# TensorE's branch behind a 448-token slot, 30 products sooner

## The chip, the cores and the metric

The kernel runs on one core of a Trainium2 chip. The metric is the device time of one execution in microseconds (us). A core has five engines with instruction queues of their own: TensorE (PE; its weight loads are listed as PEld), VectorE (DVE), ScalarE (ACT), GpSimd (POOL) and SyncE (SP), which starts most of the DMAs. A name with a q behind it (PEldq, DVEq) is an instruction that the engine's sequencer handles itself: a branch, a wait, a load of a register.

## The reference

Two steps, for 8 batches of 12 heads, 448 tokens and 64 columns per head:

```python
attn = sigmoid(q @ k.T / sqrt(64) - log(448))         # no softmax
x = (attn @ v) as [3584 tokens, 768]
e = argmax(x @ w_gate); gate_w = softmax(x @ w_gate)[e]
eom = sigmoid(x @ w_output_gate)[e]                   # of the token's expert
out = gate_w * eom * (relu(x @ w1[e]) @ w2[e])        # w1: 768 x 1024, w2: 1024 x 768
```

Each token goes to one of 8 experts. How many tokens an expert has is known only while the kernel runs.

## The kernel before

**Stages.** Up to about 268 us the kernel computes the attention, batch by batch, and at the side the gates and a list of tokens for each expert. Then it works the lists off in slots. A slot is a group of tokens of one expert: 448 (`TB`) in a full slot, 240 (`TM`) in a half slot. Two full slots take their tokens from the lists as they stand before the last batches are done, so that their loads start early; two more always follow, and up to eight more follow where the lists need them; what is left of each expert goes into half slots. With the inputs here there are seven full slots and two half slots.

**A full slot** (`slot`) has two layers. Layer 1 makes h = relu(x @ w1) in 8 parts of 128 columns. Every operand is split in a high and a low part of a shorter format, by ScalarE (high) and VectorE (low), and a product of two such operands takes three products on TensorE: L479, L480 and L481 in `products`, where the high and low part of the tokens lie side by side and the rest, which no longer fits in a bank of PSUM, is added up by VectorE in `join` (L485, L486). Layer 2 (`layer2_columns`, `layer2_turned`) makes y = h @ w2 with the columns of y as rows of PSUM, in six groups c of 128 columns; a group is 8 steps f of 3 products, 24 products, and ends with `turn_back`, in which VectorE joins the rest and turns the block (L508). Group 4 goes to `self.psy` bank 3 and group 5 to bank 4 of PSUM. The turning back of groups 4 and 5, the writing of the rows to DRAM, loading them back by token, scaling them (L555) and scattering them (L562) are left to the next slot: `finish`, a generator that the next slot calls step by step. `self.left` hands the two PSUM tiles over.

**A half slot** has layer 1 with 240 tokens, as three separate products L467, L468 and L469 for each of the 6 steps, and layer 2 the other way round (L518 to L520).

**Order.** The order of every engine's instructions is that in which the Python issues them (`manual_schedule`). The engines wait for each other by counters (semaphores), which the framework sets from the tiles that the instructions read and write.

**Branches.** Behind the four fixed full slots stand eight conditional ones, nested: each is the Else of an If (L923) whose own block is empty, so that an engine either goes on into the next slot or leaves the whole nest for the first half slot. The count of slots is read from memory by each engine (L917, and L918 for the half slots). Every engine has a branch of its own, at its own place of the stream. TensorE's stands behind the last product of layer 2 of a slot. A branch can be announced by a hint: in `layer2_columns`, ScalarE's, VectorE's and GpSimd's are marked ahead of group 2, TensorE's ahead of group 5.

```python
            for k in range(LATE_MIN, LATE_MAX):
                with tc.If(full < k + 1, label=f"big{k}", preferred_fallthrough_block=False) as none:
                    pass
                ctx.enter_context(none.Else())
...
        self.left = self.left[0], None
        with tc.manual_schedule():
            half(0)
```

With the inputs here L923 is met four times: behind the fourth full slot, the fifth and the sixth the chain goes on, and behind the seventh it is left.

Of the kernel before, what the change touches and what calls it, by code (L numbers as in the profile page):

```python
# [52 lines left out]
def r32(ap):  # L53
    return ap.bitcast(F32)


class Kernel:
# [19 lines left out]
    def memory(self):  # L77
        self.rounded = self.pool("rounded").tile([128, ROUNDED // 4], F32R, name="rounded")
        self.plain = self.pool("plain").tile([128, PLAIN // 4], F32, name="plain")
        ps = self.pool("psum", space=PSUM).tile([128, 8, 512], F32, name="ps")  # L80
        self.ps_s = [ps[:, 0:2], ps[:, 2:4]]
        self.ps_o = [[ps[:, 4], ps[:, 5]], [ps[:, 6], ps[:, 7]]]
        self.ps_s2 = ps[:, 6:8]
        self.psh = [ps[:, i] for i in (0, 1, 2)]
        self.psy = [ps[:, i] for i in (4, 5, 3)]
        self.ps_step = ps[:, 3, 0:8]
        self.rot = {}
        self.beat = [None, None]
        self.hints = {2: [ET.Activation, ET.DVE, ET.Pool]}

        c = self.carve
        w = c(0, 3, 2, 2, DF)
        self.w1s = [[w[:, d // 2, a, d % 2] for d in range(6)] for a in range(2)]
        self.w1p = [[w[:, k, a] for k in range(3)] for a in range(2)]
        self.x2 = c(12 * DF * 4, 6, 2 * TB)
        self.xs = [self.x2[:, :, TB * i:TB * i + TB] for i in range(2)]
        self.slots_begun = 0

        self.w1r = c(0, 6, DF, dt=F32)
        self.w2r = c(0, 8, DM, dt=F32)  # L100
        self.xg = c(6 * DF * 4, GB_, Q4, dt=F32)
        self.xT = c(6 * DF * 4 + XG, 6, TB, dt=F32)
        self.yq = c(6 * DF * 4 + XG, GB_, Q4, dt=F32)
        self.xTm = c(6 * DF * 4 + XG, 6, 32 * GM, dt=F32)
        self.spare = c(6 * DF * 4 + GM * Q4 * 4, DM, dt=F32), c(6 * DF * 4 + XG + 6 * 32 * GM * 4, DM, dt=F32)
# [390 lines left out]
        self.beat[0] = nc.scalar.activation(hh, ps, AF.Relu).ins  # L496
        nc.vector.scalar_tensor_tensor(hl, ps, 0.0, r32(hh), ALU.max, ALU.subtract)  # L497

    def layer2_turned(self, c):
        ps = self.take("y", self.psy)  # L500
        for f in range(8):
            wh, wl = self.w2_at(f, slice(128 * c, 128 * c + 128))
            self.products(ps, wh, wl, self.h2[:, f], f == 0, f == 7)
        return ps
# [65 lines left out]
    def slot(self, cur, nxt, side=None, begun=False, hint=None):  # L570
        nx = None
        if nxt is not None:
            nx, rows, sure = nxt() if callable(nxt) else nxt
            last = -(-nx["lx"].shape[1] // 2) - 1
        n = 32 * cur["lx"].shape[1]
        lag = 0 if self.left is not None or n == TB else 2
        fin = self.finish(n)
        next(fin, None)
        self.rot["y"] = 1
        for f in range(8):  # L580
            if begun and f == 1:
                self.change_step()
            self.layer1(f, TB if n == TB else TM, begun and f == 0)
            if nx is not None and n < TB:
                if f >= lag:
                    self.gather_rows(nx, f - lag, rows, 1)
                if f == 7 and lag == 0:
                    self.nc.gpsimd.drain()
            elif nx is not None and f <= last:
                self.gather_rows(nx, 2 * f, rows, 1)  # L590
                self.gather_rows(nx, 2 * f + 1, rows, 0)
                if f == last and not sure:
                    self.nc.gpsimd.drain()
            if f == 6 and n < TB:
                next(fin, None)
            if side is not None:
                next(side, None)
            if 1 <= f < 5:
                self.split_w2(f - 1)
                if f > 1:  # L600
                    self.load_w1(nx, f - 2)
        if lag == 0:
            for k in range(3):
                self.turn_x(nx, k)
        if n == TB:
            next(fin, None)
            self.layer2_columns(cur, nx, side, hint, fin)
            self.slots_begun += 1
            return nx
        ws = {0: (0, 1), 1: (2,)}  # L610
        for i in range(4):
            t = i // 2
            self.layer2(cur, t, i % 2, self.ys[t])
            if nx is not None:
                if lag and i == 0:
                    for g in range(8 - lag, 8):
                        self.gather_rows(nx, g, rows, g % 2)
                    self.nc.gpsimd.drain()  # L618
                for k in ws.get(i, ()):
                    self.split_w1(k)  # L620
                    for j in range(k, 4 if k == 2 else k + 1):
                        self.load_w2(nx, j)
                if lag and i == 0:
                    for k in range(3):
                        self.turn_x(nx, k)
                if i < 3:
                    self.split_x(nx, i)
            if i < 2:
                next(fin, None)
            if side is not None:  # L630
                next(side, None)
            if hint is not None and i == 1:
                self.tc.mark_branch_hint_location(hint, hint="LikelyTaken", engines=[ET.SP])
        return nx

    def layer2_columns(self, cur, nx, side, hint, fin):
        for k in range(3):
            self.split_x(nx, k)
        ps = []
        for c in range(6):  # L640
            if hint is not None and c in self.hints:
                hinted = self.hints[c]
                more = self.nc.values_load(self.more[0:1, hint[1]:hint[1] + 1], engines=hinted, min_val=0, max_val=1)
                self.tc.mark_branch_hint_location(hint[0], hint=more, engines=hinted)
            if hint is not None and c == 5:
                self.tc.mark_branch_hint_location(hint[0], hint="LikelyTaken", engines=[ET.PE])
            ps.append(self.layer2_turned(c))
            if nx is not None and c < 3:
                self.split_w1(c)
                for j in range(c, 4 if c == 2 else c + 1):  # L650
                    self.load_w2(nx, j)
            if c < 4:
                self.turn_back(ps[c], c)
            if c in (0, 2):
                next(fin, None)
            if c == 0:
                lt = cur["lt"]
                self.nc.vector.tensor_copy(self.left_at, lt[:, :, 0])
                self.nc.vector.tensor_copy(self.left_w, r32(lt[:, :, 1]))
            if side is not None:  # L660
                next(side, None)
        self.left = ps[4:], cur["lt"]

    def attention(self, pool):
        nc = self.nc
# [311 lines left out]
```

## Time and profile before

| | us |
|---|---|
| median of 3 runs | 748.69 (747.67 to 748.84) |
| the profiled execution, its own time | 748.09 |
| its span, from the first to the last instruction | 746.3 |
| TensorE busy | 738.2 (99%), 5576 products |
| VectorE, ScalarE, GpSimd busy | 449.8, 370.1, 250.3 |
| mean granted clock of TensorE | 0.998 of 2.4 GHz |

The profile is that of one execution. An engine's busy share is its work over the span; a product's time is from its start to a modelled end, and products overlap, so the distance of two starts says what one costs. The waits of an engine, and what ended them, are inferred from the counters. Where an engine's sequencer waits or branches, its work stands still or runs out of its queue, and the profile doesn't count that as busy.

### The profile page before, as it was taken

What the parts mean: (1) busy time and instruction counts of PE and PEld (TensorE: products, weight loads), DVE (VectorE), ACT (ScalarE), POOL (GpSimd) and SP (SyncE); (2) the same over time, 40 slices, a digit from 0 to 9 for tenths busy, and PEclk for the clock granted to TensorE, in tenths of its full rate; (3) what the DMA queues carried; (4) which work ended last, traced back from release to release, by engine and by line L of the source; (5) the groups of instructions that cost most, each with busy time, mean ns of one, the idle gap of its engine ahead of it and who ended that gap; (6) DMA issues with size and microseconds to landing.
All of it is one profiled execution on the core that took longest, in us unless ns stands there. A gap on an engine that the chain in (4) does not pass through costs nothing. (4 is left out here: it accounts for less than half of the span.)

```text
span 746.3 us, 14692 instructions
## 1 busy us (share of the span) xinstructions
PE 738.2 (99%) x5576; PEld 543.0 (73%) x5576; DVE 449.8 (60%) x907; ACT 370.1 (50%) x437; POOL 250.3 (34%) x375
## 2 busy tenths in 40 slices
PE   9999999999999999999999999999999999999996
PEld 4334444444344369999999999999999999999996
DVE  1343863585777849936746746746655565656555
ACT  5666666566777734404514514514514333434644
POOL 5000130032354335247525315315225234233461
PEclk9999999999999999999999999999999999999999
DMA  9464656647595765367386386476386476576951
GB/s 307 138 194 148 195 138 192 195 119 209 179 325 178 213 138 178 127 163 214 118 293 217 123 273 216 132 267 208 142 274 184 176 243 205 187 247 191 322 198 46
DMA packets 90647, 145.76 MB, mean 195 GB/s; under 512 B 16738, under 2 KB 67298, under 8 KB 90560
## 3 DMA queue, kind: packets, MB, share of 16 engines
q1 hardware_dynamic: 79808, 119.22, 51.9%
q0 software_dynamic: 9680, 24.53, 9.4%
q10 hardware_dynamic: 1072, 0.92, 0.5%
q8 instruction: 46, 0.75, 0.4%
q14 instruction: 41, 0.34, 0.1%
HBM read 118.40 MB, written 32.62 MB: 202 GB/s over the span
## 5 line engine op out<-in xcount | busy, mean ns | idle before, releaser
L709 ACT ACTIVATE a<-ps,small 128x896 f32<-128x896 f32 x168 | 168.5, 1007 | 85.2 <-PE ps L707 83.0
L707 PE MATMUL ps<-q,k 64*64 64x448 f32 x1344 | 157.1, 540 | 0.0
L716 PE MATMUL ps<-a,v 64*64 64x448 f32 x1344 | 155.8, 536 | 0.0
L389 POOL DMA_INDIRECT plain<-x_dram,lxs x112 | 111.0, 991 | 132.3 <-ACT h L496 63.2
L496 ACT ACTIVATE h<-ps 128x448 fp32r<-128x448 f32 (+1 forms) x72 | 36.5, 506 | 206.7 <-DVE ps L486 129.9
L479 PE MATMUL ps<-h,w2h 128*128 128x512 f32 x336 | 130.7, 389 | 0.0
L481 PE MATMUL ps<-h,w2l 128*128 128x448 f32 x336 | 122.6, 365 | 0.0
L479 PE MATMUL ps<-rounded 128*128 128x512 f32 x288 | 112.0, 389 | 0.0
L480 PE MATMUL ps<-h,w2h 128*128 128x384 f32 x336 | 111.9, 333 | 0.0
L707 PEld LDWEIGHTS ps<-q,k 64*64 64x64 f32 x1344 | 49.9, 134 | 76.8 <-issue 70.0
L716 PEld LDWEIGHTS ps<-a,v 64*64 64x64 f32 x1344 | 50.6, 133 | 75.7 <-issue 72.1
L481 PE MATMUL ps<-rounded 128*128 128x448 f32 x288 | 105.1, 365 | 0.0
L415 DVE TENSOR_TENSOR rounded<-plain,rounded 128x2048 fp32r<-128x2048 f32 (+5 forms) x63 | 96.4, 1566 | 10.0 <-ACT rounded L414 8.9
L480 PE MATMUL ps<-rounded 128*128 128x384 f32 x288 | 95.9, 333 | 0.0
L414 ACT CAST rounded<-plain 128x2048 fp32r<-128x2048 f32 (+5 forms) x63 | 82.0, 1333 | 24.8 <-DVE plain L434 23.6
L485 DVE COPY hb<-ps 128x64 f32<-128x64 f32 x90 | 19.8, 220 | 103.3 <-PE ps L481 86.4
L562 POOL DMA_INDIRECT out<-y,lts x24 | 42.8, 1782 | 105.3 <-ACT y L555 102.3
L481 PEld LDWEIGHTS ps<-h,w2l 128*128 128x128 f32 x336 | 63.1, 188 | 13.2
L415 DVE TENSOR_TENSOR w2l<-plain,w2h 128x768 fp32r<-128x768 f32 x72 | 65.8, 954 | 3.4 <-ACT w2h L414 0.6
L497 DVE SCALAR_TENSOR_TENSOR h<-ps,h 128x448 fp32r<-128x448 f32 (+1 forms) x72 | 41.3, 574 | 42.6 <-ACT h L496 36.1
L480 PEld LDWEIGHTS ps<-h,w2h 128*128 128x128 f32 x336 | 63.1, 188 | 4.9
L479 PEld LDWEIGHTS ps<-h,w2h 128*128 128x128 f32 x336 | 63.1, 188 | 0.0
(164 smaller groups left out, 934.6 us busy)
## 6 DMA issues: line engine op xcount, KB each, us to landing
plain<-w SPq DMA_DIRECT2D x40, 768.0 KB
plain<-w SPq DMA_DIRECT2D x27, 1024.0 KB
k<-kT SPq DMA_DIRECT2D x23, 448.0 KB
q<-qT SPq DMA_DIRECT2D x23, 448.0 KB
x_dram<-xt SPq DMA_DIRECT2D x30, 336.0 KB
v<-vm SPq DMA_DIRECT2D x23, 384.0 KB
y<-y_dram SPq DMA_DIRECT2D x18, 384.0 KB
y_dram<-plain SPq DMA_DIRECT2D x28, 192.0 KB
```

The costliest lines, as they stand in the source:

```text
L389: self.paced(self.nc.gpsimd.indirect_dma_start(out=self.xg[:, g], out_offset=None, in_=x4, in_offset=bass.IndirectOffsetOnAxis(ap=s["lx"][ ...
L414: self.nc.scalar.copy(hi, raw)
L415: self.nc.vector.tensor_tensor(lo, raw, r32(hi), ALU.subtract)
L479: mm(ps, wh, both[:, 0:512], start=first, stop=False)
L480: mm(ps[:, 512 - TB:TB], wh, both[:, 512:2 * TB], start=False, stop=False)
L481: return mm(ps[:, 0:TB], wl, both[:, 0:TB], start=False, stop=last)
L496: self.beat[0] = nc.scalar.activation(hh, ps, AF.Relu).ins
L497: nc.vector.scalar_tensor_tensor(hl, ps, 0.0, r32(hh), ALU.max, ALU.subtract)
L562: i = self.nc.gpsimd.indirect_dma_start(out=self.out, out_offset=bass.IndirectOffsetOnAxis(ap=at, axis=0), in_=y, in_offset=None, bounds_c ...
L707: qk = nc.tensor.matmul(ps[half[h], j, 0:S], k[half[j], e, o:o + 64], q[half[j], e], start=True, stop=True)
L709: self.beat[0] = nc.scalar.activation(at[u % 3], ps[:, :, 0:S], AF.Sigmoid, bias=self.bias_s, scale=1.0 / math.sqrt(D)).ins
L716: nc.tensor.matmul(self.ps_o[e][h][half[j], 0:S], v[half[h], e, c, j], a[half[h], j], start=(i in ((0, 3 if h else 4)[e],)), stop=(i == (2 ...
```

## The change

Before, a full slot issues all six groups of layer 2 and its branch stands behind them. After, the slot ends with the steps f = 0 to 5 of group 4. The steps 6 and 7 of group 4 (6 products) and the whole of group 5 (24 products) are issued at the head of the next `slot` call, whichever it is: the next full slot or the first half slot. `self.open` tells that call that a group is open and in which tile; the tile of group 5 is taken there and added to the same list that `self.left` holds. TensorE's hint is marked ahead of group 4. The order of TensorE's products stays what it was; what moves against them is the branch of L923, the register loads of L917 and L918 and the hint.

```diff
+        self.open = None
...
-    def layer2_turned(self, c):
-        ps = self.take("y", self.psy)
-        for f in range(8):
+    def layer2_turned(self, c, fs=range(8), ps=None):
+        ps = self.take("y", self.psy) if ps is None else ps
+        for f in fs:
             wh, wl = self.w2_at(f, slice(128 * c, 128 * c + 128))
             self.products(ps, wh, wl, self.h2[:, f], f == 0, f == 7)
         return ps
...
         n = 32 * cur["lx"].shape[1]
         lag = 0 if self.left is not None or n == TB else 2
+        if self.open is not None:
+            self.layer2_turned(4, range(6, 8), self.open[0])
+            self.open.append(self.layer2_turned(5))
+            self.open = None
         fin = self.finish(n)
...
-            if hint is not None and c == 5:
+            if hint is not None and c == 4:
                 self.tc.mark_branch_hint_location(hint[0], hint="LikelyTaken", engines=[ET.PE])
-            ps.append(self.layer2_turned(c))
+            if c < 5:
+                ps.append(self.layer2_turned(c, range(6) if c == 4 else range(8)))
...
-        self.left = ps[4:], cur["lt"]
+        self.open = ps[4:]
+        self.left = self.open, cur["lt"]
```

## Rows read from the trace of the kernel before

**Rows 1.** The page, part 1: busy us (share of the span) and instructions.
```profile
PE 738.2 (99%) x5576; PEld 543.0 (73%) x5576; DVE 449.8 (60%) x907; ACT 370.1 (50%) x437; POOL 250.3 (34%) x375
```

**Rows 2.** Waits of TensorE, whole span: us in total, times, longest.
```profile
PE ps L798 <- DVE small L780: 0.9, 1, 0.9
PE ps L467 <- PEq L923: 0.6, 1, 0.6
```

**Rows 3.** Timeline of TensorE, 667 to 675 us: start, us, what, idle before.
```profile
667.11 0.36 PE L481 MATMUL ps<-h,w2l 128*128 128x448 f32 x1
...
673.11 0.37 PE L481 MATMUL ps<-h,w2l 128*128 128x448 f32 x1
674.03 0.35 PE L467 MATMUL ps<-rounded 128*128 128x240 f32 x1 [0.56 <-PEq L923]
```

**Rows 4.** Windows: busy us (instructions) of PE, PEld, DVE, ACT, POOL; clock, DMA, GB/s.
```profile
674.00:740.00 66.00, 65.82 (x480) 65.53 (x480) 41.29 (x54) 38.78 (x56) 28.44 (x23) 1.00 0.59 200
```

**Rows 5.** Line 923, 480 to 660 us: duration ns min/median/max, first and last start.
```profile
L923 PEldq COMPARE_BRANCH  x3: 73/81/95, 496.9 to 612.1; - x3
```

**Rows 6.** Line 923, 660 to 667.2 us.
```profile
L923 DVEq COMPARE_BRANCH  x1: 84/84/84, 664.5 to 664.5; - x1
L923 SPq COMPARE_BRANCH  x1: 133/133/133, 664.9 to 664.9; - x1
L923 ACTq COMPARE_BRANCH  x1: 69/69/69, 665.7 to 665.7; - x1
```

**Rows 7.** Line 923, 667.2 to 675.3 us.
```profile
L923 SPq EVENT_SEMAPHORE  x9: 17/17/17, 671.0 to 675.1; - x9
...
L923 PEldq COMPARE_BRANCH  x2: 200/283/366, 669.7 to 673.7; - x2
L923 DVEq EVENT_SEMAPHORE  x2: 21/21/21, 671.2 to 671.3; - x2
L923 ACTq EVENT_SEMAPHORE  x2: 17/17/17, 671.8 to 671.9; - x2
L923 DVEq COMPARE_BRANCH  x1: 61/61/61, 671.4 to 671.4; - x1
...
L923 PEldq EVENT_SEMAPHORE  x1: 51/51/51, 673.5 to 673.5; - x1
```

**Rows 8.** Windows, 668 to 673 us, columns as in rows 4.
```profile
668.00:673.00 5.00, 5.00 (x27) 4.52 (x26) 0.00 (x0) 0.00 (x0) 0.00 (x0) 1.00 0.97 342
```

**Rows 9.** Line 467, 660 to 680 us, and the same line, 700 to 740 us.
```profile
L467 PEldq EVENT_SEMAPHORE  x1: 51/51/51, 673.9 to 673.9; - x1
...
L467 PE MATMUL ps<-rounded x48: 271/274/278, 706.9 to 722.7; 128*128 128x240 f32 x48
```

**Rows 10.** Line 508, 670 to 690 us, and the same line, 600 to 667 us.
```profile
L508 DVEq EVENT_SEMAPHORE  x5: 21/50/50, 676.2 to 676.5; - x5
...
L508 DVE STREAM_TRANSPOSE plain<-ps x10: 649/649/651, 599.8 to 664.4; 128x448 f32<-128x448 f32 x10
```

**Rows 11.** Line 917, whole span: TensorE's load of the slot count.
```profile
L917 PEldq TENSOR_LOAD <-tot x1: 509/509/509, 439.3 to 439.3; - x1
```

**Rows 12.** Branch hints (filed at line 973), 480 to 740 us.
```profile
L973 PEldq BRANCH_PREFETCH_HINT  x3: 31/31/36, 497.1 to 612.3; - x3
```

**Rows 13.** Line 485, 670 to 690 us: VectorE's first work behind the exit.
```profile
L485 DVE COPY hb<-ps x2: 186/205/224, 675.9 to 677.2; 128x64 f32<-128x64 f32 x2
```

**Rows 14.** TensorE's last product (timeline), and windows of the span's end.
```profile
739.52 0.34 PE L520 MATMUL ps<-w2h,h 128*128 128x384 f32 x1
...
742.00:743.00 1.00, 0.00 (x0) 0.00 (x0) 0.00 (x0) 0.00 (x0) 0.00 (x0) 1.00 0.63 166
743.00:744.00 1.00, 0.00 (x0) 0.00 (x0) 0.00 (x0) 0.00 (x0) 0.00 (x0) 0.53 0.31 119
```

**Rows 15.** Line 707 at the start, 3 to 5.9 us, and 6 to 12 us.
```profile
L707 PE MATMUL ps<-q,k x12: 751/951/1006, 3.8 to 5.4; 64*64 64x448 f32 x12
...
L707 PE MATMUL ps<-q,k x40: 536/536/761, 5.3 to 11.2; 64*64 64x448 f32 x40
```

## The prediction

> **What bounds the kernel now.** I read the page first: TensorE is busy for 738.2 of the 746.3 us of the span [rows 1]. Then its waits: there are two in the whole execution, 0.9 us ahead of the first product and 0.6 us at L467 behind the branch of L923 [rows 2]. So TensorE is the path, and an edit can change the time only where it opens or closes a hole in TensorE's stream. The stream around that second wait, taken product by product, is the place of this change: the last product of layer 2 starts at 673.11, the first product of the first half slot at 674.03 [rows 3]. Products of a 448-token slot follow each other every 0.20 us (30 of them lie between the starts 667.11 and 673.11 [rows 3]), so 0.92 - 0.20 = 0.72 us is lost there. Behind it TensorE works 65.82 of 66.00 us up to the last product [rows 4]: nothing downstream can take up a delay, and none is there to be won.
>
> **The branch, passed and left.** L923 is passed four times here. Three times the chain goes on; TensorE's sequencer spends 73 to 95 ns on the branch [rows 5] and the engine has no wait there [rows 2]. The fourth time all engines leave for the first half slot. That is where the engines differ, and the views of L923 before and after 667.2 us show it. VectorE takes the branch at 664.5, SyncE at 664.9, ScalarE at 665.7 [rows 6], but their first instructions in the exit block are at 671.2, 671.0 and 671.8 [rows 7]: 6.7, 6.1 and 6.1 us in which their queues are empty, while the DMA engines are 97% busy [rows 8]. TensorE's branch is at 669.7, 3.4 us ahead of its last product's start, since its sequencer runs ahead of the array; its exit block's EVENT_SEMAPHORE is at 673.5 and its second branch at 673.7 [rows 7], just behind that product's end (673.11 + 0.37 [rows 3]). So TensorE empties its queue once and goes on half a microsecond later, and comes last of the three computing engines: VectorE and ScalarE have left their exit blocks by then.
>
> **What is filed behind the meeting point.** L923 has EVENT_SEMAPHOREs at this exit alone, on each engine ([rows 7]; the view of the three other passes, [rows 5], lists branches only). I take them for the instructions that bring the engines' counters to where the skipped slots would have left them. The rows behind them fit: the first product of the first half slot has an EVENT_SEMAPHORE ahead of it, while the 48 products of the same line in the second half slot have none (the second row is all that this view has beside weight loads [rows 9]); VectorE's turn back, L508, has five of them behind the exit and none in the ten instructions ahead of it [rows 10]. So an instruction behind the meeting point waits again for operands that its engine has long known to be ready, and, by my reading, until the engine that made them has gone through its own exit block.
>
> **The change, part by part.**
> *The 30 products.* They are the same instructions in TensorE's order, 30 x 0.20 = 6.00 us, and none is added. In the unconditional slots and at the three passes that go on nothing stands between them and what follows, so they cost nothing there; what hides the branch is the sequencer's lead of 3.4 us over the array, and the price without this cover is its 0.1 us [rows 5] each time.
> *TensorE's loads of the two slot counts* (L917, L918) come ahead of the 30 products. L917 takes 509 ns [rows 11], within the same lead: nothing.
> *The hint*, set ahead of column group 4 instead of 5: the three on TensorE are filed at 497.1 to 612.3 [rows 12], that is 0.2 us behind the branches at 496.9 to 612.1 [rows 5], at the head of the slot and not where the Python marks it. Nothing.
> *No DMA and no instruction of another engine moves*; VectorE's turn back of groups 4 and 5 stands in the next slot as before.
> *The exit.* Here the order tells. TensorE now stops behind the product that starts at 667.11 [rows 3]. Its branch comes 6.0 us sooner, about 663.7. Behind the meeting point stand first group 4's products of f = 6 and 7, which read h (high part by ScalarE, low part by VectorE) and w2 (the same two engines). If they wait again as L467 does, they wait until VectorE's counter (671.2 to 671.3) and ScalarE's (671.8 to 671.9 [rows 7]) are brought up. Neither engine's arrival depends on TensorE's last 30 products: VectorE's last work ahead of its branch is the turn back of group 3. ScalarE is the later one: 671.85, and about 0.1 us from the wait to the product (673.9 to 674.03 [rows 9, 3]) gives a first product at 671.95. Lost: 671.95 - 667.11 - 0.20 = 4.64 us, in place of 0.72. Ahead of L467 nothing is lost any more, as its wait has long ended. The sum: +4.64 - 0.72 = +3.9 us.
> *Bounds of that wait.* Below: no repeated wait, or one that is met; then TensorE only drains at another place, and the change is 0 (-0.7 if the drain vanishes too). Above: it waits for the last engine's exit block, SyncE's at 675.1 [rows 7], 3.3 us past ScalarE's: +7.2 us. I take ScalarE's arrival, since the two engines that write these operands are the nearest rows; SyncE counts DMAs, and none of these operands comes by DMA.
> *What is late next.* VectorE comes to group 4's columns at 675.9 [rows 13], when they are there (671.95 + 6 x 0.20 = 673.2); group 5's come at 671.95 + 6.0 = 678.0, 0.8 us later than VectorE took them (677.2 [rows 13]), and their rows go out by DMA for work that is itself 3.9 us later. Layer 1 of the half slot starts at about 678.0 instead of 674.03, and everything behind it, the last scatter included, moves by that.
>
> The profiled execution took 748.09 us (span 746.3); 748.09 + 3.9 = 752.0. The median of the runs is 748.69, 0.6 more, so for a median I say 752.6 us. About 0.2% (1.5 us) is what a measurement here can tell from no change.
>
> **Rivals.**
> *The hole only moves* (on the other side: not slower). If group 4's last products need no wait, or TensorE's knowledge of these operands outlives the meeting point, it drains at 667.5, goes on at about 668.0, and the end stays: 748.7 us. It decides if the first product behind the exit starts before about 669.5. For it: these operands were read by TensorE itself in the same slot, for groups 0 to 3. Against it: VectorE's five repeated waits, and the wait ahead of L467 [rows 9, 10].
> *The clock falls too.* A hole of 4.6 us is new in this kernel. At the end of the span TensorE's last product ends at 739.86 (739.52 + 0.34), and the granted clock is 1.00 up to 743 and 0.53 in the microsecond behind it [rows 14], so it fell some 3.2 us after the work stopped, from 2.4 to 1.2 GHz. If that happens here, the first products behind the hole run slowly. At the start of the kernel, products of L707 up to 5.4 us took 951 ns against 536 later [rows 15], and TensorE had begun at 0.9 [rows 2]: some 4.5 to 5 us of slow work, of which half is lost. Here 1 to 2.5 us: 753.6 to 755.1 us. Against it: the hole of 0.6 us left the clock alone (1.00 behind it [rows 4]), and no row shows where between 0.6 and 3.2 us or more a fall begins. The Trainium skill, TensorE: Matmul & The Clock Gate, Part 1, says that an idle TensorE falls back to half its clock and only sustained work brings it back. By that rule the time would be this rival's; the trace agrees at the span's end.
> *TensorE's own code comes late.* Where its exit code is not at hand it meets what VectorE met: 6.7 us from branch to exit block (663.7 to 670.4, hidden by ScalarE's 671.8) and 4.5 us more from the second branch, 671.4, to 675.9 [rows 7, 13]. Then the first product starts at about 675.0 and the sum is 675.0 - 667.11 - 0.20 - 0.72 = +7.0: 755.7 us. Against it: TensorE's second branch was 0.4 us ahead of its product here [rows 7, 3], so its code was at hand. The Trainium skill, Runtime: NRT & Kernel Launch, Instruction fetch mechanics, says that a taken branch to code outside the pages held stalls until they are fetched; what the other three engines show at this exit agrees, TensorE does not.
> *Faster.* All that TensorE loses at the exit is 0.72 us, or 0.1%; I see nothing that could give 1.5 us.
>
> **How the numbers follow.** The forecast (wait for ScalarE, clock held) 0.50, own range 751.2 to 753.8; the clock falls too 0.30; late code or SyncE's count 0.07; the hole only moves 0.11; faster 0.02. The sum of the first three is slower by more than 0.2%: 0.87. Same: 0.11. The range has to hold 0.8: the forecast with its arrival uncertain by a microsecond (three engines needed 6.1 to 6.7 us), and nearly all of the clock's case: 750.6 to 755.6.
>
> **What would show it.** Right: in TensorE's stream a hole of 4.3 to 5 us between an L481 and an L479 of layer 2 near 667 to 672, ended within 0.2 us of ScalarE's EVENT_SEMAPHORE of L923; 30 products behind it and then L467 with no wait; no hole at the three earlier passes; TensorE's busy time as before (more, if the clock fell, with the granted clock at 0.50 behind the hole). Wrong: a hole of half a microsecond there, or one that ends with TensorE's own branch rather than with ScalarE's, or ScalarE's and VectorE's exit blocks at other times than 671 to 672, which would shift the sum one for one.

## The result and the profile after

| | before | after |
|---|---|---|
| median, us | 748.40 (6 runs) | 756.83 (754.26 to 758.44, 6 runs) |
| ratio | | 1.0108, 95% interval 1.0086 to 1.0129 |
| the profiled execution, its own time | 748.09 | 756.72 |
| its span | 746.3 | 754.9 |
| mean granted clock of TensorE | 0.998 | 0.993 |

The change costs 8.4 us where 3.9 were forecast, and the median lies 1.2 us above the range. In the kernel after, the lines of `products` are L480 to L482 and the If of the chain is L930.

The page, its first part, answers to [rows 1]; the waits of TensorE answer to [rows 2]:

```profile
PE 742.4 (98%) x5576; PEld 562.2 (74%) x5576; DVE 450.3 (60%) x907; ACT 369.9 (49%) x437; POOL 250.5 (33%) x375
```

```profile
PE ps L480 <- ACTq L930: 5.1, 1, 5.1
PE ps L805 <- DVE small L787: 0.9, 1, 0.9
```

TensorE is busy 4.2 us longer with the same 5576 products, and its one wait behind the exit is 5.1 us instead of 0.6. So there are two kinds of loss: waiting, and work that goes slower. The timeline of TensorE from 668 to 676 us, which answers to [rows 3], has the wait:

```profile
668.96 0.37 PE L482 MATMUL ps<-h,w2l 128*128 128x448 f32 x1
674.39 0.80 PE L480 MATMUL ps<-h,w2h 128*128 128x512 f32 x1 [5.07 <-ACTq L930]
674.99 0.52 PE L481 MATMUL ps<-h,w2h 128*128 128x384 f32 x1
```

And line 930 from 660 to 667.2 us, then from 667.2 to 678 us, which answers to [rows 6, 7]:

```profile
L930 PEldq COMPARE_BRANCH  x1: 366/366/366, 665.5 to 665.5; - x1
L930 DVEq COMPARE_BRANCH  x1: 84/84/84, 666.2 to 666.2; - x1
...
L930 ACTq COMPARE_BRANCH  x2: 49/59/69, 667.8 to 674.5; - x2
...
L930 DVEq EVENT_SEMAPHORE  x2: 21/21/21, 672.6 to 672.8; - x2
L930 ACTq EVENT_SEMAPHORE  x2: 17/17/17, 674.3 to 674.4; - x2
L930 PEldq EVENT_SEMAPHORE  x1: 51/51/51, 669.4 to 669.4; - x1
```

TensorE stands in its exit block at 669.4, just behind its last product, and could go on. Its next product starts at 674.39, 0.07 us behind the start of ScalarE's EVENT_SEMAPHORE (674.32); VectorE's, at 672.65, is passed without effect. From start to start that is 5.43 us, so 5.23 are lost, 4.51 more than before. ScalarE needed 6.5 us from its branch to this block, VectorE 6.5.

Windows of the same kernel (columns as in [rows 4]):

```profile
612.00:668.90 56.90, 56.90 (x277) 50.47 (x276) 34.24 (x59) 21.96 (x26) 19.82 (x17) 1.00 0.61 199
668.90:674.40 5.50, 0.43 (x4) 0.08 (x2) 0.00 (x0) 0.00 (x0) 0.92 (x1) 0.86 1.00 328
674.40:679.60 5.20, 5.20 (x14) 4.55 (x15) 1.10 (x3) 0.00 (x0) 0.00 (x0) 0.50 0.17 64
680.00:748.00 68.00, 68.00 (x494) 67.73 (x493) 39.57 (x51) 38.52 (x55) 28.93 (x23) 1.00 0.56 194
```

The second row is the hole, and in it the granted clock is already below 1. All six executions of the kernel after have a mean clock of 0.991 to 0.993, so the fall is not of this one alone. The third row is at 0.50, so 1.2 GHz: 14 products start in 5.20 us, where 26 would have fitted at 0.20 us each. These 12 products are 2.4 us. From 680 us on the clock is back and no hole is left.

The first row is of the slot ahead of the exit, and is full of work; but it holds 277 products, fewer than its length has room for. The windows from 613.2 to 665 us (us, PE busy, clock, DMA, GB/s) of the kernel before and of the one after say how many:

```profile
613.20:665.00 51.80, 51.80 (x261) 1.00 0.61 203
```

```profile
613.20:665.00 51.80, 51.80 (x252) 1.00 0.58 188
```

Nine products fewer in the same time, at full clock: three follow each other in 0.62 us instead of 0.60, over the whole slot. It begins at a stop of the weight loads; their timeline from 611.5 to 613.5 us:

```profile
611.85 0.19 PEld L480 LDWEIGHTS ps<-h,w2h 128*128 128x128 f32 x1
612.27 0.19 PEld L481 LDWEIGHTS ps<-h,w2h 128*128 128x128 f32 x1 [0.23 <-issue]
```

"issue" says that the load waited for nothing that the profile shows. The DMA queue q8, of the kind "instruction", has its packet of these stretches at 609.9, 3.8 us behind TensorE's branch at 606.1 (line 930, 600 to 612 us; then the DMA view, 609.5 to 610.5 us):

```profile
L930 PEldq COMPARE_BRANCH  x1: 73/73/73, 606.1 to 606.1; - x1
```

```profile
q8 instruction: 1, 0.02, 5.7%
```

I take q8 for the queue of TensorE's code, since its packets go with TensorE's stops in the runs below; no view names the engine that a queue serves. The last product ahead of the exit starts at 668.96 instead of 667.11: 1.85 us.

The sum: 4.51 (hole) + 2.4 (clock) + 1.85 (seventh slot) = 8.8 us. The last product of the span starts at 748.25 instead of 739.52 [rows 14], 8.7 us later.

### The profile page after: what moved, and what is told of

It reads as the page before. It is cut to its first block, busy times and chain, and to the rows that moved or that the text cites. A ratio compares the mean times of both kernels' runs of the same rounds, so it can differ in the third digit from the quotient of the medians.

```text
span 754.9 us, 14692 instructions
## 1 busy us (share of the span) xinstructions
PE 742.4 (98%) x5576; PEld 562.2 (74%) x5576; DVE 450.3 (60%) x907; ACT 369.9 (49%) x437; POOL 250.5 (33%) x375
## 5 line engine op out<-in xcount | busy, mean ns | idle before, releaser
L714 PE MATMUL ps<-q,k 64*64 64x448 f32 x1344 | 176.7, 537 | 0.0
L723 PE MATMUL ps<-a,v 64*64 64x448 f32 x1344 | 176.3, 536 | 0.0
L480 PE MATMUL ps<-h,w2h 128*128 128x512 f32 x336 | 132.4, 394 | 5.1 <-ACTq L930 5.1
L482 PE MATMUL ps<-h,w2l 128*128 128x448 f32 x336 | 123.7, 368 | 0.0
L723 PEld LDWEIGHTS ps<-a,v 64*64 64x64 f32 x1344 | 63.2, 133 | 67.6 <-issue 52.7
L714 PEld LDWEIGHTS ps<-q,k 64*64 64x64 f32 x1344 | 62.2, 133 | 67.8 <-issue 50.2
L480 PE MATMUL ps<-rounded 128*128 128x512 f32 x288 | 112.4, 390 | 0.0
L482 PE MATMUL ps<-rounded 128*128 128x448 f32 x288 | 105.4, 366 | 0.0
L482 PEld LDWEIGHTS ps<-h,w2l 128*128 128x128 f32 x336 | 63.7, 190 | 13.8
L480 PEld LDWEIGHTS ps<-h,w2h 128*128 128x128 f32 x336 | 63.8, 190 | 5.4 <-ACTq L930 5.4
```

What stands on the lines that cost most here:

```text
L480: mm(ps, wh, both[:, 0:512], start=first, stop=False)
L482: return mm(ps[:, 0:TB], wl, both[:, 0:TB], start=False, stop=last)
L714: qk = nc.tensor.matmul(ps[half[h], j, 0:S], k[half[j], e, o:o + 64], q[half[j], e], start=True, stop=True)
L723: nc.tensor.matmul(self.ps_o[e][h][half[j], 0:S], v[half[h], e, c, j], a[half[h], j], start=(i in ((0, 3 if h else 4)[e],)), stop=(i == (2 ...
```

## Experiments

Ratios are to the kernel before on the same chip, with 95% intervals; line numbers are each kernel's own, and the products of `products` and the If are named by their own lines there. The expectations name their theories by letters; what follows says them in words: first that TensorE waits for the later exit block of ScalarE and VectorE, with the clock's fall behind it and the slow seventh slot as costs of their own, and against it other causes of each of the three.

**Fewer products follow the branch: 12.** Group 4 and the steps 0 to 3 of group 5 stay in the slot.

```diff
-            self.layer2_turned(4, range(6, 8), self.open[0])
-            self.open.append(self.layer2_turned(5))
+            self.layer2_turned(5, range(4, 8), self.open[1])
...
-            if c < 5:
-                ps.append(self.layer2_turned(c, range(6) if c == 4 else range(8)))
+            ps.append(self.layer2_turned(c, range(4) if c == 5 else range(8)))
```

> The branch stands 12 products sooner: groups 0 to 4 and f = 0 to 3 of group 5 stay, f = 4 to 7 of group 5 follow the branch. Theory A (TensorE waits behind the exit for ScalarE's exit block, which comes at its own time, and the clock falls only in a long hole): the last product ahead of the branch starts about 670.7 us, ScalarE's block is done about 671.9, so 1.0 us is lost in place of 0.72: +0.3 us, 748.7 us, and the clock stays at 2.4 GHz. If the seventh slot also runs at 0.62 us for three products in place of 0.60, 1.9 us more: 750.6. Rival (the cost is that of products behind a branch, in proportion to their number): 12/30 of 8.4 us, +3.4 us, 751.8 us.

Measured: 748.32 against 747.14, 1.0020 [1.0009, 1.0031]. Timeline of TensorE, and the line of its If (L928):

```profile
669.22 0.37 PE L482 MATMUL ps<-h,w2l 128*128 128x448 f32 x1
672.01 0.50 PE L480 MATMUL ps<-h,w2h 128*128 128x512 f32 x1 [2.42 <-ACTq L928]
```

```profile
L928 DVEq EVENT_SEMAPHORE  x2: 21/21/21, 668.1 to 668.3; - x2
L928 ACTq EVENT_SEMAPHORE  x2: 17/17/17, 671.9 to 672.0; - x2
```

The hole is 2.79 us from start to start and ends 0.06 us behind ScalarE's block again, while VectorE has been through since 668.1. So the wait is until an arrival, not a price per product: TensorE came 2.1 us later than in the forecast (669.22 against 667.11) and waited as much less. The hole is longer than I expected, as TensorE came 1.5 us sooner than 670.7; the kernel before is 1.3 us shorter on this chip too (747.14 against 748.40), and ScalarE's block is where it was. In this trace the clock stayed and the seventh slot kept its pace, so its cost is the wait alone: 2.79 - 0.92 = 1.9 us beyond before. The median is 1.2 us over before. Three of the twelve executions took 750.2 to 751.1 us and have no trace; two of them have a mean clock of 0.995, where before has 0.997 or more, so in those the clock fell as well.

**24 products follow.** Group 4 stays whole, group 5 follows whole.

```diff
-            self.layer2_turned(4, range(6, 8), self.open[0])
             self.open.append(self.layer2_turned(5))
...
-                ps.append(self.layer2_turned(c, range(6) if c == 4 else range(8)))
+                ps.append(self.layer2_turned(c, range(8)))
```

> The branch stands 24 products sooner: groups 0 to 4 stay, group 5 follows the branch. Theory A: the last product ahead of the branch starts about 668.3, ScalarE's block is done about 671.9 to 672.5, so 3.4 to 4.0 us are lost in place of 0.72: +2.7 to 3.3 us, 751.1 to 751.7 us with the clock kept; with the clock fallen about 2.4 us more, 753.5 to 754.1, and up to 1.9 us more if the seventh slot runs at 0.62 us for three products. Rival (in proportion to the products): 24/30 of 8.4, +6.7 us, 755.1 us, with the clock up or down.

Measured: 755.40 against 747.14, 1.0111 [1.0097, 1.0126]: no better than 30, and above what was expected. Timeline of TensorE in the seventh slot and at the exit, windows, and the line of the If:

```profile
611.38 0.39 PE L480 MATMUL ps<-h,w2h 128*128 128x512 f32 x1
613.83 0.68 PE L481 MATMUL ps<-h,w2h 128*128 128x384 f32 x1 [2.05 <-issue]
...
673.28 0.37 PE L482 MATMUL ps<-h,w2l 128*128 128x448 f32 x1
676.06 0.47 PE L480 MATMUL ps<-h,w2h 128*128 128x512 f32 x1 [2.41 <-DVEq L929]
```

```profile
613.90:617.20 3.30, 3.30 (x9) 0.50 0.20 79
618.00:665.00 47.00, 47.00 (x229) 1.00 0.54 176
```

```profile
L929 ACTq EVENT_SEMAPHORE  x2: 17/17/17, 674.9 to 675.0; - x2
L929 DVEq EVENT_SEMAPHORE  x2: 21/21/21, 675.9 to 676.0; - x2
```

The stop in the seventh slot is 2.4 us here, and q8's packet, at 611.5, is 4.9 us behind the branch (606.6). Half clock follows, and then the pace of 0.62 us (229 products in 47.0 us, where the pace of before, 261 in 51.8 us, gives 237). At the exit VectorE is the later one for once, and its block ends the hole; that hole, of 2.8 us, leaves the clock alone. So the stop behind a passing branch is a cost of its own.

**The hole filled.** Eight fp32 products of 448 columns are added to the empty block of the exit, on TensorE alone.

```diff
+    def fill(self):
+        for f in range(8):
+            self.nc.tensor.matmul(self.psh[0][:, 0:TB], r32(self.w2_at(f, slice(0, 128))[0]), r32(self.h2[:, f, 0:TB]), start=(f == 0), stop=(f == 7))
...
                 with tc.If(full < k + 1, label=f"big{k}", preferred_fallthrough_block=False) as none:
-                    pass
+                    with tc.manual_schedule():
+                        self.fill()
```

> The changed kernel with eight products of 448 columns on operands that TensorE has already read, into a free bank of PSUM, in the exit's own block (their result is not used). They fill part of the hole and hold nothing up. Theory A: the hole still ends with ScalarE's exit block; the clock does not fall, so the products behind it start 0.20 us apart and not 0.37: 2.4 us less than the changed kernel, 754.4 us. Rival (the slow products behind the hole are not the clock's, but of the cold code or of the operands): the same time as the changed kernel, 756.8 us, or more by the added work, with slow products behind the exit.

Measured: 754.23 against 747.14, 1.0098 [1.0084, 1.0113]; the profiled execution 752.75. Windows of TensorE, and the two ends of the wait:

```profile
666.00:672.50 6.50, 6.04 (x17) 1.00 0.99 342
672.60:745.00 72.40, 71.98 (x510) 1.00 0.53 184
```

```profile
665.66 0.36 PE L486 MATMUL ps<-h,w2l 128*128 128x448 f32 x1
...
672.58 0.50 PE L484 MATMUL ps<-h,w2h 128*128 128x512 f32 x1 [0.54 <-ACTq L934]
```

With work in the hole the clock never falls, and the first product behind it still starts just behind ScalarE's block (672.5). In this trace the seventh slot kept its pace (q8's packet 3.3 us behind the branch). From the last product ahead of the exit to the first of the 30 are 6.92 us, 6.0 more than before, and the profiled execution is 5.6 us over before on its chip: that is the wait without the two other costs. The median, 7.1 us over before, is above that; the three other executions (753.37 to 755.28) have no trace, but their clock of 0.998 to 0.999 says that it was not the clock's fall that they lost beyond it.

**The code shifted.** 30 more tiny products (8 columns) at 272 us put all later instructions of TensorE 60 places further; they take 0.8 us themselves.

```diff
-                self.change_step()
+                self.change_step(32)
```

> The changed kernel with 30 tiny products (8 columns) more in the first full slot, which move every later instruction of TensorE's code back by 60 places, to where the branches stood before. Theory A for the seventh slot (a page of TensorE's code comes late there, about 6 us behind the third branch, and the stream falls out of its step): the seventh slot keeps 0.60 us for three products, no weight load is late near 612 us; 1.9 us less for that and 1 to 2 us more for the tiny products: 755.9 to 757 us, the trace deciding. Rival (the slower pace comes with the early branch itself): 0.62 us for three products in the seventh slot again, 758 to 759 us.

Measured: 755.01 against 747.14, 1.0109 [1.0094, 1.0124]. Windows and timeline of TensorE:

```profile
613.20:665.00 51.80, 51.80 (x261) 1.00 0.59 193
672.30:678.00 5.70, 5.70 (x15) 0.50 0.21 86
```

```profile
666.86 0.37 PE L482 MATMUL ps<-h,w2l 128*128 128x448 f32 x1
672.24 0.79 PE L480 MATMUL ps<-h,w2h 128*128 128x512 f32 x1 [5.01 <-ACTq L930]
```

No late weight load, 261 products again, and still a hole of 5.38 us and the fall behind it. In this trace the seventh slot's loss is gone and the exit's is not. That the place of the code did it is not shown: two runs below lose nothing there with TensorE's code where the change has it.

**ScalarE and VectorE told to leave.** Before and after, their hint takes a value from memory, which says whether the chain goes on. Here it is the constant "LikelyTaken", like TensorE's. It also comes sooner: it is filed just behind the branch ahead of the slot (605.9 us on VectorE, 607.5 on ScalarE), while the value's hint of that slot stood at 661.1 and 652.3 us in the trace after, 5.1 and 15.6 us ahead of the branch.

```diff
-                hinted = self.hints[c]
+                self.tc.mark_branch_hint_location(hint[0], hint="LikelyTaken", engines=[ET.Activation, ET.DVE])
+                hinted = [ET.Pool]
```

> The changed kernel with a fixed hint for the exit on ScalarE and VectorE at the head of each conditional slot, in place of the one read from memory late in the slot. Theory A (the hole lasts until ScalarE and VectorE have fetched their exit code): with the code at hand their exit blocks stand half a microsecond behind their branches, as GpSimd's do, at 665 to 666.5 us; TensorE goes on 0.5 to 1 us behind its own drain, the clock stays, and the time is that of the kernel before, 747.1 to 747.9 us, plus 0 to 2 us if a page of TensorE's code comes late in the seventh slot. If the early hint does not last until the branch, the exit blocks and the time stay as in the changed kernel, 1.011 times the kernel before. Rival (TensorE is held by its own exit, not by the others): ScalarE's and VectorE's blocks come early and the hole stays 5 us.

Measured: 747.01 against 746.88, 1.0003 [0.9994, 1.0013]. Line 931 (the If), TensorE's waits and windows:

```profile
L931 DVEq COMPARE_BRANCH  x2: 61/66/72, 663.4 to 664.2; - x2
...
L931 ACTq COMPARE_BRANCH  x2: 49/52/54, 664.8 to 665.8; - x2
...
L931 DVEq EVENT_SEMAPHORE  x1: 21/21/21, 664.1 to 664.1; - x1
L931 ACTq EVENT_SEMAPHORE  x1: 17/17/17, 665.7 to 665.7; - x1
L931 PEldq EVENT_SEMAPHORE  x1: 51/51/51, 666.5 to 666.5; - x1
```

```profile
PE ps L480 <- PEq L931: 0.6, 1, 0.6
```

```profile
667.00:733.00 66.00, 65.98 (x478) 65.46 (x479) 36.71 (x49) 34.26 (x49) 26.59 (x22) 1.00 0.64 223
```

This is the run that decides. The 30 products still follow the branch, but ScalarE is in its exit block 1.0 us behind its branch and VectorE 0.7, ahead of TensorE. The hole is 0.93 us from start to start, as before, the clock holds, and the whole loss is gone. Placing the products behind the branch costs nothing by itself; what costs is that ScalarE and VectorE come late to the meeting point. The two other engines come late here as well, SyncE at 670.2 and GpSimd at 672.2 us, 6.4 behind its branch where it was 0.5 before and after, and TensorE waits for neither. Whether the constant or the earlier place of the hint makes the exits early, this run doesn't tell.

**No loads of weights in the conditional slots.** The loads of w2 there are left out.

```diff
-                    self.load_w2(nx, j)
+                    if hint is None:
+                        self.load_w2(nx, j)
```

> The changed kernel without the loads of w2 for the next slot in the conditional slots (their layer 2 then works on old weights, so the output is not the reference's). Theory A, with the DMA engines' load as what makes the exit code late: ScalarE's and VectorE's exit blocks come some 3 us behind their branches, as at the end of the span, not 6 to 7; the hole is 1 to 2 us in place of 5.4, the clock stays, and the time is 0.5 to 1.5 us above the kernel before, plus 0 to 2 us for the seventh slot. Rival (the fetch takes 6 us whatever the DMA engines do): a hole of 5 us and 7 to 8 us above the kernel before.

Measured: 747.98 against 746.88, 1.0016 [1.0006, 1.0026]. Line 931, and the timeline of TensorE:

```profile
L931 DVEq EVENT_SEMAPHORE  x2: 21/21/21, 666.8 to 666.9; - x2
L931 ACTq EVENT_SEMAPHORE  x2: 17/17/17, 667.3 to 667.4; - x2
```

```profile
667.41 0.50 PE L480 MATMUL ps<-h,w2h 128*128 128x512 f32 x1 [1.49 <-ACTq L931]
```

With the DMA engines 43% busy at the exit (663 to 667.4 us), where they were 97 to 100%, ScalarE takes 2.8 us from branch (664.57) to block, where it took 6.1 before and 6.5 after. The hole shrinks to 1.86 us. So much of the lateness of ScalarE's exit code is load on the DMA. For VectorE that isn't shown: it takes 3.9 us here, but 4.0 to 7.4 in the other traces without its constant hint.

**The kernel before with its code shifted.** The second slot leaves out its last 30 products, so TensorE's code lies 60 places nearer, with the branch where it was.

```diff
...
-            ps.append(self.layer2_turned(c))
+            ps.append(self.layer2_turned(c) if self.slots_begun != 1 or c < 4 else self.layer2_part(c))
```

> The kernel before, whose second full slot leaves out the last 30 products of layer 2 (its output is then not the reference's): the branches stay where they were, and TensorE's code behind them moves up by the 60 places by which the change moves it. 6.0 us less for the products left out. Theory A for the seventh slot (the place of the page in the code): a late weight load near 606 to 612 us and 0.62 us for three products in some executions, 741.1 to 743 us, as in the changed kernel; the exit as before, 0.7 us. Rival (the early branch itself slows the seventh slot): 0.60 us throughout, 741.1 us.

Measured: 741.62 against 746.88, 0.9925 [0.9908, 0.9942]: 5.3 us less, for 6.0 us of products left out. No late load and no slow slot in its trace: there the shift alone made none.

**TensorE's hint left out.**

```diff
-            if hint is not None and c == 4:
-                self.tc.mark_branch_hint_location(hint[0], hint="LikelyTaken", engines=[ET.PE])
```

> The changed kernel without TensorE's hints. Theory A for the seventh slot (the hint behind each branch keeps the next page of TensorE's code from being fetched in time): no late weight load, 0.60 us for three products throughout; at the exit TensorE now fetches its own code too, 6 to 7 us behind its branch, which is hidden where ScalarE and VectorE take as long: 0 to 2 us less than the changed kernel, 1.008 to 1.011 times the kernel before. Rival (the hint has no part in it): the seventh slot is as in the changed kernel, in some executions slow.

Measured: 755.61 against 746.88, 1.0120 [1.0103, 1.0137]. Line 928 (the If, 600 to 667.2 us), and the timeline and windows of TensorE:

```profile
L928 PEldq COMPARE_BRANCH  x3: 64/197/3693, 604.9 to 666.5; - x3
...
L928 PEldq EVENT_SEMAPHORE  x1: 51/51/51, 666.3 to 666.3; - x1
```

```profile
665.89 0.37 PE L482 MATMUL ps<-h,w2l 128*128 128x448 f32 x1
673.52 0.80 PE L480 MATMUL ps<-h,w2h 128*128 128x512 f32 x1 [7.26 <-ACTq L928]
```

The seventh slot now has no late load and 261 products in the window, q8's packets come at 584.2 and 610.8 and hold nothing up; the price is a branch of 3.7 us at the exit (3693 ns), which TensorE's lead hides (its block is 3.8 us behind the branch, as in the trace of before). But TensorE is then only earlier at the same wait: 7.63 us from start to start, to ScalarE's block at 673.4. Without the seventh slot's loss, this trace is no cheaper.

**ScalarE alone told to leave.** As in the run with both, but VectorE keeps its value.

```diff
-                hinted = self.hints[c]
+                self.tc.mark_branch_hint_location(hint[0], hint="LikelyTaken", engines=[ET.Activation])
+                hinted = [ET.DVE, ET.Pool]
```

> The changed kernel with the fixed exit hint at the head of the slot on ScalarE alone; VectorE and GpSimd keep the late one. Theory A (the hole ends with the later of ScalarE's and VectorE's exit blocks): ScalarE's block comes within 1 us of its branch, VectorE's 4 to 7 us behind its own, so the hole ends with VectorE's, at 668 to 672 us: 2 to 5 us lost in place of 0.7, with 2.4 us more where the clock falls: 748.5 to 753.5 us by a kernel before of 747. Rival (ScalarE's block alone holds TensorE): the time of the kernel before, 747 us, and a hole of 0.9 us.

Measured: 753.77 against 747.80, 1.0076 [1.0054, 1.0097]. Timeline of TensorE:

```profile
667.20 0.37 PE L482 MATMUL ps<-h,w2l 128*128 128x448 f32 x1
672.08 0.77 PE L480 MATMUL ps<-h,w2h 128*128 128x512 f32 x1 [4.52 <-DVEq L931]
```

ScalarE's block is at 666.7, and now the hole ends with VectorE's (671.9). Both engines hold TensorE up, and in the program both write the operands; taking away the later one only uncovers the other, with a hole of 4.88 us from start to start instead of 5.43 to 6.08 in the traces of the change. The clock falls here too.

**The changed kernel, two more traces.**

> The changed kernel once more, for one more trace. Theory A for the seventh slot (the page of TensorE's code that is asked for behind the third branch comes late or not by chance): the page is asked for 2 to 5 us behind the branch at about 606 us; where that is under about 3.5 us the seventh slot runs at 0.60 us for three products without a stop, where it is over, a weight load is late and the slot goes on at 0.62. The exit as in the first trace: a hole of about 5 us that ends with ScalarE's or VectorE's block, and the clock at half for some microseconds. Rival: a slow seventh slot without a late page, or a late page without a slow slot.

> The changed kernel a third time, as for the run before: the seventh slot slow or not with the time of the page, the exit as in the first trace.

Measured: 755.26 and 756.00, beside 747.80. Timeline of TensorE in the first of them:

```profile
672.96 0.80 PE L480 MATMUL ps<-h,w2h 128*128 128x512 f32 x1 [5.54 <-ACTq L930]
```

The holes from start to start are 5.91 (667.05 to 672.96) and 6.08 us (667.60 to 673.68), each ending less than 0.1 us behind ScalarE's block, with half clock behind them. Both have the late weight load in the seventh slot (q8's packet 4.1 and 3.9 us behind the branch), but lose 0.3 us by it and then keep 0.60 us for three products: the window from 613.2 to 665 us has 261 in the first of them. My theory that the slow pace follows each late load fell here. The load comes late in all three traces of the change and in two more (24 products; ScalarE's hint); the slow pace came behind it in two of these five. What decides it stays open.

The other half of the theory held. With the branch 24 or 30 products sooner and TensorE's hint in place, q8's packet came 3.8 to 4.9 us behind the third branch in the five traces with the late load, and 1.2 to 3.3 us behind it in the four where no load is late (fill, shift, both hints, no weight loads). The runs with both hints and without weight loads touch no instruction of TensorE, so the load can be on time with its code and hint as the change has them.

## Why the prediction was wrong

The direction and the wait were right. The size was not: three costs were left out of the sum or made too small.

**Right: the wait and who ends it.** "If they wait again as L467 does, they wait until VectorE's counter" and ScalarE's "are brought up". In ten traces (all of kernels with products behind the branch but the one with both hints) the first product starts 0.06 to 0.2 us behind the later of these two blocks, whichever it is, and with both early (the run with constant hints) nothing is left of the 8.4 us. SyncE's block, at 672.9 to 677.1 in the trace after, plays no part. That an instruction waits for these two because they wrote its operands is my reading of this; the traces show whom it waits for. The rival that the hole only moves is out.

**The step that failed most: "clock held".** The forecast's sum stops at +3.9, and the clock's fall was a rival with 0.30. In the traces it fell in every one of the six holes at the exit of 4.9 us and more, and held behind the five of 2.8 us or less in the runs of variants. Its size, 2.4 us, is the upper end of the 1 to 2.5 that I worked out from the kernel's start; so the case that should have been the sum is this one, at about 755. The row that spoke for it [rows 14] has the fall some 3.2 us after work ends, sooner than the 4.6 us that I forecast; the hole of 0.6 us that I set against it says nothing of one so long. The Trainium skill, TensorE: Matmul & The Clock Gate, Part 1, has an idle TensorE fall back to half its clock; the trace agrees, with 0.50 from 674.4 to 679.6 us.

**The hints and the passing branches, priced at nothing.** At the passes that go on, "nothing stands between them and what follows" is true of operands, but TensorE's weight load can stop there, as I read it because the instructions behind the branch are fetched late: 0.3 us in two traces of the change, and 1.85 us with the slow pace behind it in the first. I had that rival, but only for the exit, where TensorE was on time in every trace. In the trace without TensorE's hint no load comes late behind the passing branch, and in the one with the code shifted by 60 places none does either. But none does in two traces that keep both the place of the code and the hint, so neither is shown to be the cause. What the nine traces show is that the load is late where q8's packet is (3.8 us and more behind the branch, as the hint stands in them); why the packet is late stays open. The Trainium skill, Runtime: NRT & Kernel Launch, Instruction fetch mechanics, has code fetched ahead in sequence and a taken branch break this. The exits of ScalarE and VectorE agree (6.5 us each).

**The term of the wait, mis-sized.** The sum's "first product at 671.95" took ScalarE's block from one trace. From TensorE's last product ahead of the exit to its first one behind it were 4.84 us by that, and 5.43, 5.91 and 6.08 in the three traces of the change: lost beyond before are 4.5 to 5.2 us, not 3.9. ScalarE took 5.8 to 7.0 us from branch to block in the traces without its constant hint and with all loads, and its branch moves against TensorE's stream too.

**The sums.** In the profiled execution: forecast +3.9; the wait 0.6 more, the clock 2.4, the seventh slot 1.85; together +8.8 against +8.6 measured. In the two later traces it is mostly wait and clock: 5.0 + 2.4 + 0.3 = 7.7 and 5.2 + 2.4 + 0.4 = 8.0, against 7.5 and 8.2 over before on their chip. The range ended at 755.6, as it had the clock's fall with the wait of one trace and nothing for the seventh slot.

## What to carry to other kernels

Work that was moved behind a point where all engines meet waited here for the later of the two engines that made its operands, though TensorE had long read these operands. Read from the trace when each of them gets through its exit, over several executions, before moving anything past it. If work has to stand there, first make the other engines' exits early (here a constant hint at the head of the slot: ScalarE's 5.8 to 7.0 us became 1.0). And where a forecast opens a hole in TensorE's stream longer than any that the kernel has, the fall of the clock behind it belongs in the sum and not beside it.

## What was not expected of the hardware

- The way out of a branch costs ScalarE 5.8 to 7.0 us with the DMA engines 96% busy or more from its branch to its exit block, 2.8 without the weight loads, and 1.0 with a constant hint at the head of the slot.
- At full clock the stream of products can settle at 0.62 us for three instead of 0.60 after a stop, and keep that to the next stop: 252 products against 261 in 51.8 us. Two of five late loads led to it.
- The stop need not be at the exit for the clock to fall: the 2.4 us in the seventh slot (24 products) were followed by half clock, while 2.8 us at the exit of the same execution were not.
